# Turning the first two units' inputs on TensorE, one tile for the filler products, and instruction orders planned backwards and forwards, in a fused gated-linear-attention and MLP kernel

## The chip, the core and the metric

The kernel runs on one core of one Trainium2 chip. The metric is the device time of one launch in microseconds. All data is float32 on the chip; the two weight matrices arrive as 64-bit floats and are rounded to float32 by the kernel itself. In this document TensorE is PE, VectorE is DVE, ScalarE is ACT, GpSimd is POOL, and SyncE, which here only issues DMAs, is SP.

## The reference

A gated linear recurrence over 4 batches and 8 heads, 768 positions of 48 features each, and behind it a two-layer MLP on 3072 tokens:

```python
state = np.zeros((B, H, D, D))                      # B 4, H 8, S 768, D 48
for t in range(S):
    state = alpha[:, :, t, :, None] * state + np.einsum('bhd,bhe->bhde', k[:, :, t], v[:, :, t])
    y[:, :, t] = np.einsum('bhd,bhde->bhe', q[:, :, t], state)
x = y.transpose(0, 2, 1, 3).reshape(B * S, H * D)   # 3072 x 384
h = x @ w_in                                        # 384 x 2048
g = h - np.tanh(h)
out = g @ w_out                                     # 2048 x 384
```

## The kernel before

The 3072 tokens are cut into 12 **units** of 256 positions; a unit has two **chunks** of 128. For each unit the attention part (`gla`) makes the features `xT`, and the MLP part (`moe`) runs 8 **steps**, each of 256 hidden features: `first` (the product with `w_in`, tile `h`), `square`, `quad`, `cube`, `shrunk` (a polynomial for `h - tanh(h)`), and `second` (the product with `w_out`, tile `o`). Units 0 and 1 (`PLAIN = 2`) do `second` in the plain way while the weights are still coming in; later units use seven half-size products instead of eight, with combinations of the blocks of `w_out` (`combos`, tiles `b` and `e`).

Every piece of work is a task with an engine, an estimated duration, a rank and a list of tasks it needs. A planner lays the tasks out, and each engine then runs its own list strictly in that order:

```python
class Planner:
    def add(self, name, engine, us, rank, after, do, lat=0.25): ...
    def order(self):
        ...
        while any(open_.values()):
            at, engine = min((max(free.get(e, 0.0), min(ready[i] for i in ts)), e)
                             for e, ts in open_.items() if ts)
            i = min((i for i in open_[engine] if ready[i] <= at), key=lambda i: (self.tasks[i][3], i))
            ...            # the task of least rank among those that are ready
        return sorted(done, key=lambda x: x[:2])
```

The recurrence wants the features on the partitions and the positions along the row. alpha, k and q lie in memory the other way round, so they are loaded in rows of 1536 bytes into 32 partitions per half (`raws`), widened by ACT and transposed in 32 x 32 blocks by DVE:

```python
def load(u, what):                                  # what: 0 alpha, 1 k, 2 q, 3 v
    queue = A if u == 0 and what in (1, 3) else nc.sync
    if what == 3: ...                               # v, rows of 192 bytes, one DMA per chunk
    t, x = raws[what], (alpha, k, q)[what]
    for hh in range(2):
        src = x[b].rearrange("(g two) s d -> two g (s d)", two=2)[hh][:, t0 * D:(t0 + TU) * D]
        queue.dma_start(out=t[HP * hh:HP * hh + 32].rearrange("p g r d -> p g (r d)"),
                        in_=src.rearrange("g (i n) -> i g n", i=32))

def widen(what):                                    # ACT, two copies
    ...
def flip(what, make):                               # DVE, four 128x256 transposes
    t = make()
    for g in range(NP):
        V.transpose(t[:, g].rearrange("p c (i r) -> p r c i", r=R), raws[what][:, g, :, 0:32])
```

From the turned alpha two scans make the running products `U` (backwards) and `W` (forwards); k is multiplied by `U` (`kU`) and q by `W` (`qW`). Each chunk then has these tasks on PE, with DVE and ACT between them: `scores` (tile `sc`), `back` (tile `tp`, k turned back), `y`, `update` (tile `up`, what is added to the state). The features of a chunk are 8 heads x 48 = 384 = 3 x 128, but a pair of heads fills only 2 x 48 of 128 partitions; the last two heads fill the gaps of 16 partitions in the three tiles. In units 0 and 1 (`direct`) TensorE computes these gaps itself, with small products from `v_gap` and `s_gap`; in the other units the last two heads go into a fourth block, and six small DMAs (`moves`) bring them into the gaps:

```python
direct = u < PLAIN
def products():
    y = m["y", c] = bank("y")
    to_gap = [(hh, slice(HP * hh + D - gap, HP * hh + HP), j)
              for hh in range(2) for j in range(KT)] if direct else []
    rows = P if direct else HP + D
    if n > 0:
        for g in range(KT if direct else NP):
            T.matmul(y[0:rows, g, :], lhsT=old[:, g, 0:rows], rhs=m["qT"][:, g, c, :], ...)
        for hh, at, j in to_gap:
            T.matmul(y[at, j, :], lhsT=s_gap[quads[hh], j, :], rhs=m["qT"][quads[hh], NP - 1, c, :], ...)
    for hh, at, j in to_gap:
        T.matmul(y[at, j, :], lhsT=v_gap[:, c, hh, j, :], rhs=m["pm", c][hh][:, NP - 1, :], ...)
    for g in range(KT if direct else NP):
        for hh, q in enumerate(quads):
            T.matmul(y[q, g, :], lhsT=vts[u][:, c, 2 * g + hh, :], rhs=m["pm", c][hh][:, g, :], ...)
```

The weights come in 16 pieces, each 786 KB as 64-bit words, through four `raw` buffers; ACT reads a piece (two activations) and DVE rounds it (two instructions). Until there is real work, PE multiplies the identity with itself (`spin`):

```python
RANK = {"in": -3, "out": 8}
pieces = [("in", 0), ("in", 1)]
for s in range(FS):
    pieces += [("out", s)] + ([("in", s + 2)] if s + 2 < FS else [])
...
add("spin 0", "PE", 9, -99, [], lambda: spin(36))
add("spin 1", "PE", 1.5, -20, [f"qT 0"], lambda: spin(7))
```

At the end a flag `ok` is computed from the size checks on the data; where it fails, a slower general kernel runs. With the reference's inputs it does not run.

Of the kernel before, what the change touches and what calls it, by code (L numbers as in the profile page):

```python
# [317 lines left out]
class Planner:  # L318

    def __init__(self):
        self.tasks = []

    def add(self, name, engine, us, rank, after, do, lat=0.25):
        self.tasks.append((name, engine, us, rank, [a for a in after if a], do, lat))

    def order(self):
        names = {t[0]: i for i, t in enumerate(self.tasks)}
        assert len(names) == len(self.tasks)  # L330
        needs = [[names[a] for a in t[4]] for t in self.tasks]
        users = [[] for _ in self.tasks]
        for i, ns in enumerate(needs):
            for j in ns:
                users[j].append(i)
        left = [len(ns) for ns in needs]
        ready = [0.0] * len(self.tasks)
        free, open_ = {}, {}
        for i, t in enumerate(self.tasks):
            if not left[i]:  # L340
                open_.setdefault(t[1], []).append(i)
        done = []
        while any(open_.values()):

            at, engine = min((max(free.get(e, 0.0), min(ready[i] for i in ts)), e)
                             for e, ts in open_.items() if ts)
            i = min((i for i in open_[engine] if ready[i] <= at), key=lambda i: (self.tasks[i][3], i))
            open_[engine].remove(i)
            _, _, us, _, _, do, lat = self.tasks[i]
            free[engine] = at + us  # L350
            done.append((at, len(done), do, i))
            for j in users[i]:
                ready[j] = max(ready[j], at + us + lat)
                left[j] -= 1
                if not left[j]:
                    open_.setdefault(self.tasks[j][1], []).append(j)
        assert len(done) == len(self.tasks)
        return sorted(done, key=lambda x: x[:2])


def fast(tc, q, k, v, alpha, moe_w_in, moe_w_out, out, w_in, w_out, ident, ok, pad_rows):
# [17 lines left out]
    with ExitStack() as ctx:  # L379
# [12 lines left out]
        for t, x in zip(raws, (1.0, 0.0, 0.0)):  # L392
            for hh in range(2):
                V.memset(t[HP * hh + 32:HP * hh + HP, :, :, D - 32:32], x)

# [37 lines left out]
        RANK = {"in": -3, "out": 8}  # L433
# [15 lines left out]
        pieces = [("in", 0), ("in", 1)]  # L449
        for s in range(FS):  # L450
            pieces += [("out", s)] + ([("in", s + 2)] if s + 2 < FS else [])
        raw_of = {}

# [12 lines left out]
        for n, (what, s) in enumerate(pieces):  # L466
            rank = RANK[what] + 2 * s
            held = pieces[n - 4] if n >= 4 else None
            add(f"fetch {what}{s}", "SP", 3.9, rank - 30, [held and f"read {held[0]}{held[1]}"],
                lambda what=what, s=s: fetch(what, s), lat=2.5)  # L470
            a, b = convert(what, s)
            older = pieces[n - 2] if n >= 2 else None
            add(f"read {what}{s}", "ACT", 2.1, rank, [f"fetch {what}{s}", older and f"{older[0]}{older[1]}"], a)
            add(f"{what}{s}", "DVE", 1.6, rank, [f"read {what}{s}"], b)
# [4 lines left out]
        def load(u, what):  # L479

            b, i = divmod(u, UPB)
            t0 = i * TU
            queue = A if u == 0 and what in (1, 3) else nc.sync
            if what == 3:
                vt = vts[u] = two.tile([P, CU, H, D], FP32, name="vt")
                for c in range(CU):
                    queue.dma_start(out=vt[:, c],
                                    in_=v[b, :, t0 + c * P:t0 + (c + 1) * P, :].rearrange("h p d -> p h d"))
                return
            t, x = raws[what], (alpha, k, q)[what]  # L490
            for hh in range(2):
                src = x[b].rearrange("(g two) s d -> two g (s d)", two=2)[hh][:, t0 * D:(t0 + TU) * D]
                queue.dma_start(out=t[HP * hh:HP * hh + 32].rearrange("p g r d -> p g (r d)"),
                                in_=src.rearrange("g (i n) -> i g n", i=32))

        def gla(u, rank):
# [6 lines left out]
            direct = u < PLAIN  # L503
# [6 lines left out]
            for what, name in enumerate(("aT", "kT", "qT", "v")):  # L510
                go(f"load {name}", "SP", 2.3, -9 + 0.1 * what, [prev and what < 3 and f"{name}{prev}"]
                   + [f"{last} {u - 2}.{CU - 1}" for last in ("y", "state") if what == 3 and u > 1
                      and (last == "y" or (u - 2) % UPB < UPB - 1)],
                   lambda what=what: load(u, what), lat=2.5)

            def widen(what):
                for hh in range(2):
                    t, r0 = raws[what], HP * hh
                    to, of = t[r0 + 32:r0 + HP, :, :, 0:D - 32], t[r0:r0 + 32, :, :, 32:D]
                    if u == 0 and what == 0 and hh == 1:  # L520
                        V.tensor_copy(to, of)
                    else:
                        A.copy(to, of)
# [6 lines left out]
            def new(name):  # L530
# [3 lines left out]
                     lambda: new("kT"), lambda: new("qT"))  # L534
            for what, (name, k_) in enumerate((("aT", 0), ("kT", 2), ("qT", 4))):
                go(f"wide {name}", "ACT", 1.25, k_ - 0.5, [f"load {name}"], lambda what=what: widen(what))
# [10 lines left out]
            def ends():  # L547
# [4 lines left out]
                V.tensor_reduce(out=least[:, u:u + 1], in_=U[:, :, 0], axis=AX.X, op=ALU.min)  # L552
                V.reciprocal(before[:, 0::P + 1], e)

# [14 lines left out]
            go("U", "DVE", 2.3, 1, ["aT", prev and f"kU{prev}", prev and f"sizeU{prev}"], scan_U)  # L569
            go("ends", "DVE", 0.5, 3, ["U"], ends)  # L570
            go("W", "DVE", 2.3, 3, ["ends", prev and f"qW{prev}", prev and f"sizeW{prev}"], scan_W)
            go("kU", "DVE", 1.2, 3, ["kT", "U"], lambda: scale("kT", "U"))
            go("qW", "DVE", 1.2, 5, ["qT", "W"], lambda: scale("qT", "W"))
# [3 lines left out]
            def bank(name):  # L577


                if direct:  # L580
                    return ps_o.tile([P, NP, P], FP32, name=name, tag="o2" if name == "y" else "o3")
                return ps_sc.tile([P, NP, P], FP32, name=name, tag="sc0" if name == "y" else "sc1")

            def chunk(c):
# [25 lines left out]
                def masked():  # L610
                    pm = m["pm", c] = [two.tile([P, NP, P], FP32, name=f"pm{hh}", bufs=1) for hh in range(2)]
# [16 lines left out]
                def products():  # L628
                    y = m["y", c] = bank("y")
# [28 lines left out]
                def back():  # L658
                    tp = m["tp", c] = bank("tp")
# [7 lines left out]
                def update():  # L667
                    up = m["up", c] = bank("up")[:, :, 0:2 * D].rearrange("p g (two d) -> p g two d", d=D)
# [4 lines left out]
                def state():  # L673
                    for hh, q in enumerate(quads):
                        if n == 0:
                            V.tensor_copy(new[q, :, q], m["up", c][q, :, hh, :])
# [7 lines left out]
                kU, qW = f"kU {u}", f"qW {u}"  # L684
                go_c("scores", "PE", 1.2, 7, [kU, qW] + held, scores)
                go_c("masked", "DVE", 1.3, 8, ["scores", past and f"y {past}"], masked)
                if n > 0:
                    go_c("decay", "DVE", 0.6, 6, [f"ends {u}", f"state {past}"], decay)
                if direct:
                    go_c("gaps", "ACT", 0.9, 7, [f"load v {u}", n > 0 and "decay", past and f"y {past}"], gaps)  # L690
                go_c("y", "PE", 2.2 if n else 1.2, 9,
                     ["masked", f"load v {u}", n > 0 and "decay", direct and "gaps",
                      direct and past and f"x {past}"], products)
                go_c("x", "ACT", 0.6 if direct else 1.5, 10, ["y"], features)
                if not last:
                    go_c("back", "PE", 0.6, 6 if direct else 8.5,
                         [kU, None if direct else "masked", direct and past and not past_last and f"state {past}"], back)
                    go_c("natural", "ACT", 0.6, 9, ["back"], natural)
                    go_c("update", "PE", 1.15, 9.5, ["natural", f"load v {u}"], update)
                    go_c("state", "DVE", 0.8, 10,  # L700
# [40 lines left out]
        for n in range(5):  # L741
            add(f"combine {n}", "DVE", 1.7, 2 * FS + 1 + n,
                [f"out{FS - 1}", f"in{FS - 1}", f"gaps {PLAIN - 1}.{CU - 1}", f"y {PLAIN - 1}.{CU - 1}"]
# [18 lines left out]
        def moe(u, rank, gait):  # L762
# [3 lines left out]
            def step(s):  # L766
# [16 lines left out]
                def square():  # L783
                    if s % 2 == 0:
                        m["us"] = two.tile([P, 2, 2 * TU], FP32, name="u")
                    m["u", s] = m["us"][:, s % 2]
# [15 lines left out]
                def large():  # L802
                    big = two.tile([P, N * (P + 1)], FP32, name="big", tag="junk", bufs=1)[:, 0:4 * TU]
                    n = (u * FS + s) // 2
                    A.activation(big, m["us"].rearrange("p s t -> p (s t)"), AF.Relu, bias=-U_FAST, scale=W_SCALE,  # L805
# [9 lines left out]
                def second():  # L815
# [27 lines left out]
                    + [f"x {u}.{c}" if plain else f"moves {u}" for c in range(CU if plain else 1)], first)  # L843
# [50 lines left out]
        def spin(n):  # L894

            t = ps_o.tile([P, P], FP32, name="spin", tag="o0")
            for _ in range(n):
                T.matmul(t, lhsT=ident, rhs=ident, start=True, stop=True)
        add("spin 0", "PE", 9, -99, [], lambda: spin(36))
        add("spin 1", "PE", 1.5, -20, [f"qT 0"], lambda: spin(7))  # L900

# [28 lines left out]
        add("judge", "DVE", 1.2, 16 * NU, [f"large {last_step}", f"x {NU - 1}.{CU - 1}"] + [f"look {n}" for n in range(len(pieces))], judge)  # L930
# [73 lines left out]
```

## Time and profile before

| what | value |
|---|---|
| time, median of 3 runs | 622.51 us (618.29 to 622.78) |
| the profiled run | 617.95 us, span 616.2 us |
| PE busy | 596.8 us (97%), 3717 matmul instructions |
| DVE busy | 463.4 us (75%) |
| ACT busy | 342.5 us (56%) |
| POOL busy | 4.5 us (1%) |
| HBM read / written | 44.04 MB / 4.72 MB |
| chain that ended last, by engine | PE 92%, DMA 3%, DVE 2%, issue 1% |

The table is read from the top down: one engine is busy for almost the whole span, and the chain of work that ended last, which is followed back from the last instruction, runs over the same engine for 92% of the span. A group in the profile is named by what it writes and reads: `h<-xT,w_in` is the product with the first weight matrix. Each float32 matmul of the program appears as two instructions (for instance the 576 products `first` as 1152 records). "PEclk" is the granted share of the TensorE clock, 1.00 being full.

### The profile page before, as it was taken

The page shows a single profiled execution, that of the slowest core. Times are in us where ns is not written, and L with a number is a line of the kernel's source. Part 1 is how long each engine was busy: PE and PEld are TensorE (multiplying, and loading weights), DVE is VectorE, ACT ScalarE, POOL GpSimd, SP SyncE. Part 2 cuts the span into 40 slices and gives each one's busy share as a digit, 9 for nine tenths or more (in the row PEclk, how much of TensorE's full clock was granted, in tenths as well). Part 3 has the DMA queues.
Part 4 walks back from the last instruction along what each step waited for, and adds up shares of the span by engine and source line. Part 5 has one row for each costly group of instructions (what it writes and reads, how often), then busy time and mean ns, then how long its engine had stood idle before and what let it go on. Part 6 is the DMA issues. An engine that isn't in the chain of part 4 may idle for free.

```text
span 616.2 us, 9861 instructions
## 1 busy us (share of the span) xinstructions
PE 596.8 (97%) x3717; PEld 529.5 (86%) x3717; DVE 463.4 (75%) x885; ACT 342.5 (56%) x633; POOL 4.5 (1%) x18
## 2 busy tenths in 40 slices
PE   7689999999999999999999999999999999999994
PEld 7578776777999899999999999899899998999994
DVE  7997599997995896985895895786796744635652
ACT  3777898486877666676564564454444433333430
POOL 2000000000000000000000000000000000000000
PEclk9799999999999999999999999999999999999998
DMA  9996991445565275472040030030010000000001
GB/s 172 201 192 171 236 208 52 103 112 152 114 153 125 81 133 123 111 159 76 31 105 1 28 84 25 27 85 27 27 32 1 27 7 1 27 7 1 26 1 32
DMA packets 55161, 50.48 MB, mean 82 GB/s; under 512 B 29056, under 2 KB 44864, under 8 KB 55104
## 3 DMA queue, kind: packets, MB, share of 16 engines
q1 hardware_dynamic: 52448, 48.78, 34.3%
q10 hardware_dynamic: 2656, 0.98, 1.0%
q8 instruction: 31, 0.51, 0.4%
q14 instruction: 26, 0.21, 0.1%
HBM read 44.04 MB, written 4.72 MB: 79 GB/s over the span
## 4 chain that ended last, share of the span: by engine, by line
PE 92%; DMA 3%; DVE 2%; issue 1%; ACT 0%; ACTq 0%; SPq 0%; DVEq 0%
PE h L778 40%; PE o L838 30%; PE o L823 7%; PE sc L607 4%; PE y L646 4%; PE y L635 3%; DMA raw<-in_moe_w_in_dram 3%; PE up L670 2%; PE tp L661 1%; DMA kr<-in_k_dram 1%; DVE qT L528 1%; PE y L642 1%; DVE qT L563 0%; DVE W L558 0%; PE y L638 0%
## 5 line engine op out<-in xcount | busy, mean ns | idle before, releaser
L778 PE MATMUL h<-xT,w_in 128*128 128x256 f32 x1152 | 266.2, 381 | 0.6 <-ACT xT L652 0.6
L778 PEld LDWEIGHTS h<-xT,w_in 128*128 128x128 f32 x1152 | 215.9, 191 | 29.9 <-ACT xT L652 0.8
L787 ACT ACTIVATE u<-h 128x512 f32<-128x512 f32 x96 | 57.3, 596 | 205.4 <-PE h L778 204.9
L795 DVE TENSOR_TENSOR w<-h,u 128x512 f32<-128x512 f32 x96 | 66.1, 688 | 80.0 <-ACT u L787 79.9
L838 PE MATMUL o<-b,e 128*128 128x192 f32 x480 | 91.1, 326 | 0.0
L838 PE MATMUL o<-w_out,e 128*128 128x192 f32 x320 | 80.9, 335 | 0.0
L838 PEld LDWEIGHTS o<-b,e 128*128 128x128 f32 x480 | 80.2, 190 | 0.0
L799 DVE SCALAR_TENSOR_TENSOR g<-z,w 128x512 f32<-128x512 f32 x96 | 65.9, 687 | 10.7 <-ACT z L791 5.9
L838 PE MATMUL o<-b,g 128*128 128x192 f32 x320 | 65.1, 326 | 0.0
L838 PEld LDWEIGHTS o<-w_out,e 128*128 128x128 f32 x320 | 56.2, 190 | 6.9 <-issue 3.0
L791 ACT ACTIVATE z<-u 128x512 f32<-128x512 f32 x96 | 60.4, 629 | 2.3
L838 PEld LDWEIGHTS o<-b,g 128*128 128x128 f32 x320 | 54.2, 190 | 0.0
L805 ACT ACTIVATE big<-u 128x1024 f32<-128x1024 f32 x48 | 50.1, 1045 | 0.0
L823 PE MATMUL o<-w_out,g 128*128 128x384 f32 x128 | 44.0, 489 | 0.0
L823 PEld LDWEIGHTS o<-w_out,g 128*128 128x128 f32 x128 | 23.9, 190 | 14.3 <-issue 0.4
L811 DVE TENSOR_TENSOR e<-g 128x256 f32<-128x256 f32 x80 | 33.4, 418 | 2.4
L812 DVE TENSOR_TENSOR e<-g 128x256 f32<-128x256 f32 x80 | 33.4, 417 | 0.0
L607 PEld LDWEIGHTS sc<-qT,kT 48*128 48x128 f32 x368 | 23.4, 195 | 10.0 <-issue 5.2
L613 DVE TENSOR_TENSOR pm<-sc,mask 128x512 f32<-128x512 f32 x46 | 29.5, 683 | 3.2 <-PE sc L607 3.2
L607 PE MATMUL sc<-qT,kT 48*128 48x128 f32 x368 | 28.0, 294 | 2.4 <-DVE qT L563 2.4
L544 DVE TENSOR_TENSOR_SCAN U<-aT,after 128x1032 f32<-128x1032 f32 x12 | 27.5, 2294 | 0.3
L558 DVE TENSOR_TENSOR_SCAN W<-aT,before 128x1032 f32<-128x1032 f32 x12 | 27.6, 2302 | 0.0
(100 smaller groups left out, 617.9 us busy)
## 6 DMA issues: line engine op xcount, KB each, us to landing
raw<-in_moe_w_out_dram SPq DMA_DIRECT2D x16, 768.0 KB, 5.6
raw<-in_moe_w_in_dram SPq DMA_DIRECT2D x32, 288.0 KB, 6.6
ar<-in_alpha_dram SPq DMA_DIRECT2D x24, 192.0 KB, 3.4
qr<-in_q_dram SPq DMA_DIRECT2D x24, 192.0 KB, 3.3
kr<-in_k_dram SPq DMA_DIRECT2D x22, 192.0 KB, 4.9
vt<-in_v_dram SPq DMA_DIRECT2D x22, 192.0 KB, 4.1
raw<-in_moe_w_in_dram SPq DMA_DIRECT2D x32, 96.0 KB, 6.8
out_dram<-same SPq DMA_DIRECT2D x20, 96.0 KB, 1.7
```

The source lines that it names most:

```text
L607: T.matmul(sc[hh][:, g, :], lhsT=m["kT"][q, g, c, :], rhs=m["qT"][q, g, c, :], start=True, stop=True)
L613: V.tensor_mul(pm[hh], m["sc", c][hh], mask.unsqueeze(1).to_broadcast([P, NP, P]))
L778: T.matmul(h[:, a, :], lhsT=w_in[:, j, f * P:(f + 1) * P], rhs=xT[u][:, j, :], start=(j == 0), stop=(j == KT - 1))
L787: A.activation(m["u", s], m["h", s], AF.Square, scale=W_SCALE ** -1.5)
L791: A.activation(m["z", s], m["u", s], AF.Square, bias=QB, scale=QA * W_SCALE)
L795: V.tensor_mul(m["w", s], m["h", s], m["u", s])
L799: V.scalar_tensor_tensor(out=g.rearrange("p a c t -> p (a c t)"), in0=m["z", s], scalar=QK, in1=m["w", s], op0=ALU.add, op1=ALU.mult)
L805: A.activation(big, m["us"].rearrange("p s t -> p (s t)"), AF.Relu, bias=-U_FAST, scale=W_SCALE, accum_out=over[:, n:n + 1])
L811: V.tensor_add(e[:, 0:2, :], g[:, 0], g[:, 1])
L812: V.tensor_sub(e[:, 2:4, :], g[:, :, 1, :], g[:, :, 0, :])
L823: T.matmul(m["o"][c], lhsT=g[:, a, c, :], rhs=w_out[:, f, :], start=(f == 0), stop=(f == FT - 1))
L838: T.matmul(o[n][:, i], lhsT=g_, rhs=w_, start=(s == 0 and (n, i) in ((0, 0), (1, 0), (2, 1), (3, 0))), stop=(s == FS - 1), skip_group_chec ...
```

## The change

Its parts, and what each is for:

1. **alpha, k and q of unit 0 and k and q of unit 1 turned by TensorE** (`TURNED`). They are loaded in rows of 384 bytes (two positions of one head), 128 partitions at once (`rough`), one DMA each. PE multiplies each head's 64 columns with the identity, which turns them into PSUM: 8 matmuls for the even and 8 for the odd positions (`turn`). alpha is copied from PSUM (even half by ACT, odd half by DVE); k and q are multiplied by `U` and `W` straight out of PSUM, in two halves. This takes the place of `widen` on ACT and of four transposes on DVE for each of the five tensors.
2. **The second unit's gaps through DMAs**: `direct` holds for unit 0 alone. Unit 1 uses the fourth block and the six `moves`.
3. **All filler products into one tile**: the matmuls that only keep PE busy are 40 single tasks (`SPINS`), all into one PSUM tile `o2`, that the planner puts wherever PE would stand idle before the first `y`.
4. **The order**: the planner runs eight rounds. It plans forwards, turns the plan round to find how late each task may end, plans forwards again with those times as priorities (with some noise in later rounds), and keeps the shortest plan by its own estimates. An engine may also wait for a more urgent task that will soon be ready.
5. **Around it**: pieces of weights sorted by rank with `RANK["out"] = 3`; other estimates of durations; `least` taken out of `ends`; the first state copied by ACT instead of DVE; separate `pm` tiles for the second chunk of unit 0; other PSUM banks for the tasks of units 0 and 1; v's second half in unit 0 alone on ACT's queue.

The diff, cut to its core:

```diff
 class Planner:
+    ROUNDS, SEED, NOISE = 8, 1, 2.0
     def order(self):
-        ... one forward pass, least rank first ...
+        chance = random.Random(self.SEED)
+        priority, late, best = [t[3] for t in self.tasks], None, None
+        for n in range(self.ROUNDS):
+            starts, order = self.run(priority, before, after, late if n % 2 else None)
+            ends = [s + t[2] for s, t in zip(starts, self.tasks)]
+            if best is None or max(ends) <= best[0]:
+                best = max(ends), starts, order
+                turned, _ = self.run([-e for e in ends], after, before)
+                back = [r + t[2] for r, t in zip(turned, self.tasks)]
+                fair = [max(back) - b for b in back]
+            late = fair if n < 4 else [x + chance.gauss(0, self.NOISE) for x in fair]
+            priority = late
...
+        TURNED = ((0, 1, 2), (1, 2))
+        def by_matmul(u, what):
+            return u < len(TURNED) and what in TURNED[u]
...
-        RANK = {"in": -3, "out": 8}
+        RANK = {"in": -3, "out": 3}
-        pieces = [("in", 0), ("in", 1)]
-        for s in range(FS):
-            pieces += [("out", s)] + ([("in", s + 2)] if s + 2 < FS else [])
+        pieces = sorted(((what, s) for s in range(FS) for what in RANK), key=lambda x: (RANK[x[0]] + 2 * x[1], x))
+        SPINS = 40
... load():
+            if by_matmul(u, what):
+                if u > 0:
+                    make_rough(u, what)
+                (A if u == 0 and what == 1 else nc.sync).dma_start(
+                    out=rough[u, what][:, 0:BOTH].rearrange("p (h n) -> p h n", h=H),
+                    in_=x[b, :, t0:t0 + TU, :].rearrange("h (p two) d -> p h (two d)", two=CU))
+                return
... gla():
-            direct = u < PLAIN
+            direct = u == 0
+            def turn(what, n):
+                ...
+                t = m["turned", what, n] = pool.tile([P, NP, P], FP32, name="turned", tag=tag)
+                for h in range(H):
+                    at = (h * CU + n) * D
+                    T.matmul(t[HP * (h % 2):HP * (h % 2) + HP, h // 2, :], lhsT=rough[u, what][:, at:at + HP], rhs=ident,
+                             start=True, stop=True)
+            def place(n):
+                (V.tensor_copy if n else A.copy)(each(tail[:, :, 0:P], n), turned(0, n))
+            def times(what, by, n):
+                ...
+                V.tensor_mul(each(m[name].rearrange("p g c t -> p (g c) t"), n), turned(what, n), each(m[by][:, :, 1:], n))
...
-                            V.tensor_copy(new[q, :, q], m["up", c][q, :, hh, :])
+                            A.copy(new[q, :, q], m["up", c][q, :, hh, :])
...
-        add("spin 0", "PE", 9, -99, [], lambda: spin(36))
-        add("spin 1", "PE", 1.5, -20, [f"qT 0"], lambda: spin(7))
+        for n in range(SPINS):
+            add(f"spin {n}", "PE", 0.29, 99, [n > 0 and f"spin {n - 1}"], spin, lat=0.0)
```

From the order of the instructions in the changed program, without its times: PE runs 17 fillers, the turns of alpha and k, 1 filler, the turn of q, 4 fillers, `back` 0.0, 4 fillers, `update` 0.0, 7 fillers, both `scores` of unit 0, `back` 0.1, 7 fillers, `y` 0.0, `update` 0.1, `y` 0.1, the four turns of unit 1, and then the first two products with `w_in`. (0.1 is chunk 1 of unit 0.) The matmuls of the whole program change by 80 turns, 24 gap products fewer, 4 more products with `vt`, 2 more with `state` and 3 fillers fewer (43 to 40).

## The prediction, made before the changed kernel ran

> **What bounds the kernel now.** I read the page's forty slices first, to see where the busiest engine is not busy; then the table of windows over the start; then TensorE's timeline there; then the waits.
>
> ```profile
> PE   7689999999999999999999999999999999999994
> ...
> PEclk9799999999999999999999999999999999999998
> ```
>
> A slice is 15.4 us. PE is full from the fourth slice to the last but one, with the clock at full. The waits of PE between 60 and 600 us are an empty list, and PE is busy for 50.00 of 50.00 us in each window from 100 us on. So what remains after about 46 us is a fixed amount of PE work, and the end moves only by what PE idles, wastes or runs slowly before it, by PE work added or taken away, and by new stalls. The last matmul ends at 608 us; behind it lie 8 us of output that the change leaves alone.
>
> ```profile
> 10.00:15.00 5.00, 2.55 (x23) 2.36 (x23) 4.96 (x10) 1.32 (x3) 0.00 (x0) 1.00 1.18 177
> 15.00:20.00 5.00, 2.87 (x26) 2.68 (x26) 4.86 (x7) 3.46 (x5) 0.00 (x0) 1.00 1.08 180
> 20.00:25.00 5.00, 3.59 (x33) 3.42 (x33) 3.93 (x6) 2.03 (x3) 0.00 (x0) 0.57 1.08 201
> 25.00:30.00 5.00, 3.78 (x34) 2.54 (x30) 4.71 (x10) 4.84 (x9) 0.00 (x0) 0.75 1.23 212
> ...
> 45.00:50.00 5.00, 5.00 (x23) 4.21 (x22) 4.01 (x9) 2.96 (x7) 0.00 (x0) 0.70 0.08 18
> ```
>
> The columns are length, busy PE, weight loads, DVE, ACT, POOL, granted clock, DMA share, GB/s. From 10 to 20 us PE is half idle while DVE is full (4.96 and 4.86 of 5): DVE turns alpha, k and q. Then the clock falls to 0.57 and 0.75, and once more to 0.70 at 45 us. The DMA engines are full too.
>
> ```profile
> 1.52 10.91 PE L898 MATMUL spin<-ident 128*128 128x128 f32 x72 [1.52 <-POOL ident masks.py:199]
> 14.87 0.66 PE L661 MATMUL tp<-ident,kT 128*128 128x128 f32 x4 [2.45 <-DVE kT L563]
> ...
> 21.66 2.08 PE L607 MATMUL sc<-qT,kT 48*128 48x128 f32 x16 [1.41 <-DVE qT L563]
> ...
> 31.73 1.09 PE L638 MATMUL y<-qT,s_gap 48*32 48x128 f32 x12
> 32.75 1.09 PE L642 MATMUL y<-pm,v_gap 128*32 128x128 f32 x12
> ...
> 35.21 5.45 PE L778 MATMUL h<-xT,w_in 128*128 128x256 f32 x24 [0.58 <-ACT xT L652]
> ...
> 43.88 1.50 PE L607 MATMUL sc<-qT,kT 48*128 48x128 f32 x16 [1.03 <-DVE qT L563]
> ...
> 46.21 3.63 PE L778 MATMUL h<-xT,w_in 128*128 128x256 f32 x12
> ```
>
> A line is start, duration, engine, what, count and, in brackets, the idle time and its releaser. The scores of unit 0 wait for q until 21.66 us; the first product with `w_in` starts at 35.21. The useful work before it is only about 10 us: `back` and `update` twice (2.5), two `scores` (2.1 at full clock), `y` 0.0 (1.8), `y` 0.1 (3.5). So some 25 us at the start are waits, fillers and slow clock. After it PE waits twice (0.73 and 1.03 us), and twelve records of `h` take 3.63 us where twelve elsewhere take 2.59.
>
> **What the Trainium skill says.** The page "TensorE: Matmul & The Clock Gate", Part 1, says that the clock is at half until about 3.4 us of steady work, and falls back after an idle window. The trace agrees: 0.57 between 20 and 25 us, after idle gaps of 2.45, 2.13 and 1.41 us. It is why fillers between the real matmuls should help. Part 3 of that page says that matmuls in different row or column groups run side by side. The trace has the row kind: 16 records of `sc` with 48 rows, 8 matmuls of the program, take 1.16 us, so 145 ns each, against 303 ns for a filler (10.91/36). The turns write 64 columns at partitions 0 and 64 alternately; I give 8 of them and 8 scores 1.05 us a group (an estimate: 1.16 less the overlap of about 0.1 with the next group), which no trace here shows yet for the turns. "DMA: Bandwidth & Descriptors", Specifications, asks for transfers of 512 bytes or more for full rate. The trace shows the cost as smooth: in the DMA view from 6.8 to 8.6 us ACT's queue has 543 packets, nearly all rows of 192 bytes, in 38.8% of 16 x 1.8 us, so 20.6 ns each; from 2.5 to 6.8 us 276 packets of 1340 bytes on average in 39.6% of 16 x 4.3 us, so 99 ns each. A straight line between gives 34 ns for 384 bytes (estimate).
>
> **The change part by part.**
>
> Loads: alpha and k share the engines. Before, 2 x 256 packets of 1536 bytes at 112 ns over 16 engines are 3.6 us; after, 2 x 1024 at 34 ns are 4.35. alpha was there at 6.4 us, so now at about 7.2, and q 2.2 us later at 9.4. This part costs 0.8 us.
>
> DVE and ACT: 5 tensors x 2.03 us of transposes go (10.2), one widening copy (0.42) and the first state copy (0.73) too; in come one copy from PSUM (0.65) and eight half products at 0.7 for four whole ones at 1.2 (+0.8). DVE: -9.9 us. ACT: nine widening copies of 0.62 go (-5.6), and the gaps of unit 1 (-1.5); in come the other half of alpha (0.65), the state copy (0.7) and unit 1's features in two kinds of copies (0.26 + 0.47, four times, for 2 x 0.48: +2.0). ACT: -3.8 us. Neither is the bound, so this counts only where PE waits for it.
>
> PE, in the order that the changed program has, at full clock: 17 fillers end at 1.5 + 17 x 0.3 = 6.7; alpha at 7.2; turns of alpha and k 4.2: 11.4; filler 0.3 and turn of q 2.1: 13.8; 4 fillers: 15.0; `back` 0.45, 4 fillers, `update` 0.8: 17.45; 7 fillers: 19.55; two `scores` 2.1: 21.65; `back` 0.45: 22.1; 7 fillers: 24.2; `y` 0.0 1.85, `update` 0.8, `y` 0.1 3.5: 30.35; four turns of unit 1 4.2: 34.55. DVE keeps up: turned alpha at 9.3, copy 0.65 with its waits 10.1, `U` 2.3: 12.4, both halves of k and `ends`: 14.2 (`back` comes at 15.0), `W`: 16.5, q: 18.0 (`scores` come at 19.55). So the first `h` starts at **34.6 us**, hardly earlier than 35.2. The waste ahead of it falls from 25 us to 34.6 - 10 - 10.5 = 14, so by 11, but ten turn groups bring 10.5 us of new work. The fillers, 12 us of them, stand fixed in the queue and are a wait of their own where DVE is ready sooner.
>
> After it the same work is shorter. Before, from 35.2 to the end of the fifth `h` and the second `o` at 69.45: 34.2 us. After: five `h` (13.1), two `o` (5.2), two `scores` (2.1), two `back` (0.9), two `update` (1.6), two `y` of unit 1 without gap products (4 and 8 matmuls, 0.93 + 1.0, so 3.9): 26.8 us. The difference of 7.4 is 3.1 for the gap products (2 x (1.02 + 1.02), less 1.0 for the fourth block), 1.8 for the two waits, 1.5 for the slow `h` and `sc`, and about 1 for other slow or broken runs. PE arrives at this mark at 34.6 + 26.8 = 61.4 instead of 69.45: **8 us earlier**. Behind the mark the work is the same in both.
>
> **The rivals.**
>
> *Weights become the bound.* Three pieces of `w_in` were issued in 12.4 us, so 4.1 each; at the 248 GB/s of 60 to 80 us a `w_out` piece takes 3.2. From q at 9.4: v 2.6, seven `w_in` pieces 28.7, alpha, q, k, v of unit 1 8.9, three `w_out` 9.6 give 59.2 us for the seventh `w_in`; reading and rounding add 4: 63. PE wants it at 66.5. The margin is 3 us; if the four buffers or ACT (9.80 of 10 us busy from 90 to 100 us) break the stream, 2 to 5 us of the gain are lost: 615 to 618.
>
> *DVE becomes the bound.* It is 97 to 99% busy from 80 to 140 us. But it loses 9.9 us of work, more than PE gains, so the ratio stays. I give it 10%.
>
> *The turns or loads are slower.* The path holds ten turn groups: 0.1 us more each is 1 us; alpha 1 us later is 1 us.
>
> *More gain than counted.* The profiled run is 4 us below the median; if the ordinary run loses more to the slow clock in the gaps, and the steadier stream of fillers removes that, the gain against the median is 10 to 12 us.
>
> *The new order stalls PE later.* In both orders `second` of a step follows two to three `first` behind in nearly every step; I see nothing that gets tighter.
>
> **Range and chances.** 622.5 - 8.0 = 614.5; the last rival but one pulls it down by 2: 612.5. With weights as the bound 618; with a fully steady clock 606. Faster by 2% means under 610.1, which needs 12.4 us: 0.33. Slower by 2% would need a stall that nothing points to: 0.03.
>
> **What would show it.** Right: first `h` at 33 to 36 us; PE's clock at 0.95 or more up to 50 us; no gap products at 50 and 58 us; the end of the second `o` near 61 us; empty PE waits behind it. Wrong: PE waiting for `w_in` or `w_out` between 55 and 85 us; `turned` groups over 1.3 us; alpha later than 8 us; or the first `h` well under 33 us, which would mean that the turns cost less than I say.

## The result, and the profile after

| | median | range | runs |
|---|---|---|---|
| before | 621.4 us | 618.29 to 622.78 | 4 |
| changed | 611.51 us | 611.02 to 611.95 | 4 |

The ratio is 0.985, with an interval of 0.981 to 0.989: 9.9 us by the medians. That is likely the upper end of what the change is worth. In the three later sets, with 11 to 46 runs each, the kernel before had medians of 617.3, 617.8 and 617.9 us. The two profiled runs lie 6.0 us apart (spans of 616.2 and 610.2 us). The changed kernel itself was not run in those sets, but the kernel nearest to it there, the changed one with the old planner, lay 5.2 us under the kernel before of its own set (612.08 against 617.32). Taken together, the change saves about 6 us, and 10 only against that first set; the 6 is inferred across sets.

The forty slices of the page after, PE and its clock:

```profile
PE   9999999999999999999999999999999999999994
...
PEclk9999999999999999999999999999999999999998
```

Before, the first three slices held a 7, a 6 and an 8 and the clock a 7: now PE is full from the first slice on, at full clock. Part of that is filler. The windows of the changed kernel (length, busy PE, weight loads, DVE, ACT, POOL, clock, DMA share, GB/s):

```profile
10.00:15.00 5.00, 5.00 (x78) 4.54 (x75) 4.29 (x6) 1.51 (x4) 0.00 (x0) 1.00 1.11 212
15.00:20.00 5.00, 5.00 (x53) 4.87 (x53) 4.50 (x7) 3.00 (x6) 0.00 (x0) 1.00 1.21 187
20.00:25.00 5.00, 4.89 (x62) 4.41 (x62) 4.64 (x11) 4.85 (x10) 0.00 (x0) 1.00 1.16 235
```

PE's timeline of the changed kernel (start, duration, engine, line, what, count; idle time before it and its releaser in brackets):

```profile
1.51 6.91 PE L1028 MATMUL spin<-ident 128*128 128x128 f32 x34 [1.51 <-POOL ident masks.py:199]
8.35 3.71 PE L613 MATMUL turned<-ident,rough 128*64 128x128 f32 x64
...
19.17 1.16 PE L732 MATMUL sc<-qT,kT 48*128 48x128 f32 x16
...
33.24 5.45 PE L906 MATMUL h<-xT,w_in 128*128 128x256 f32 x24
...
41.97 2.42 PE L906 MATMUL h<-xT,w_in 128*128 128x256 f32 x10 [0.70 <-DVE w_in L87]
...
59.20 2.75 PE L906 MATMUL h<-xT,w_in 128*128 128x256 f32 x12
...
68.26 2.42 PE L906 MATMUL h<-xT,w_in 128*128 128x256 f32 x10 [0.71 <-DVE w_in L87]
...
600.24 1.14 PE L966 MATMUL o<-b,e 128*128 128x192 f32 x6
```

Two lines of the kernel before, to compare with (its second `o`, and its last group of matmuls):

```profile
66.71 2.74 PE L823 MATMUL o<-w_out,g 128*128 128x384 f32 x8
...
606.82 1.14 PE L838 MATMUL o<-b,e 128*128 128x192 f32 x6
```

The turns start with no idle time before them: PE came to them late because it was still at its 17 fillers. The two longer waits left are for a rounded piece of `w_in` (line 87 is the second rounding instruction). The fifth `h` starts at 59.20 and ends at 61.95, with two `o` done by then: that is the mark of the prediction, reached at 69.45 us before. PE's last matmul ends at 601.38 us, and at 607.96 before.

### The profile page after: what moved, and what is told of

Same layout as the page of the kernel before. It is cut to its first block, busy times and chain, and to the rows that moved or that the text cites. A ratio compares the mean times of both kernels' runs of the same rounds, so it can differ in the third digit from the quotient of the medians.

```text
span 610.2 us, 10100 instructions
## 1 busy us (share of the span) xinstructions
PE 598.1 (98%) x3835; PEld 531.8 (87%) x3835; DVE 452.9 (74%) x866; ACT 341.3 (56%) x633; POOL 4.4 (1%) x18
## 3 DMA queue, kind: packets, MB, share of 16 engines
q1 hardware_dynamic: 56688, 49.07, 35.2%
## 4 chain that ended last, share of the span: by engine, by line
PE 96%; DMA 1%; DVE 1%; SPq 0%; issue 0%; ACT 0%; POOL 0%; DVEq 0%; POOLq 0%
PE h L906 40%; PE o L966 30%; PE o L951 7%; PE sc L732 4%; PE y L775 4%; PE y L764 3%; PE up L799 3%; PE spin L1028 2%; PE tp L790 1%; DMA raw<-in_moe_w_in_dram 1%; PE turned L613 1%; PE y L771 0%; DVE w_in L87 0%; SPq L43 0%; DVE same L1007 0%
## 5 line engine op out<-in xcount | busy, mean ns | idle before, releaser
L732 PE MATMUL sc<-qT,kT 48*128 48x128 f32 x368 | 26.7, 285 | 0.0
```

Source lines behind the costliest of these rows:

```text
L732: T.matmul(sc[hh][:, g, :], lhsT=m["kT"][q, g, c, :], rhs=m["qT"][q, g, c, :], start=True, stop=True)
```

## The experiments

Twelve kernels ran. The number after "Measured" is the median, with the range in brackets, of four runs where no other number is given. The kernel before in the same sets had 617.79 (15 runs), 617.9 (46) and 617.32 us (11). "More" and "less" are against the changed kernel's 611.51 us, which comes from the first set; its medians are compared across sets, so differences of about 1 us are not certain, and the traces are read beside them. In the runs that alter what is turned, the gaps or the planner, the planner also lays out a new order, so they compare whole plans.

### Do the fillers help, or stand in the way?

Four runs. The first three keep the changed kernel's order and only leave fillers out:

```diff
-            add(f"spin {n}", ..., spin, lat=0.0)
+            add(f"spin {n}", ..., (lambda n=n: spin() if KEEP(n) else None), lat=0.0)
# e1: KEEP is never; e2: not 8 <= n < 17; e2b: 8, 1, 2, 2, 3, 3 of 17, 1, 4, 4, 7, 7
```

**No fillers.** 

> The changed kernel with its order kept, but none of the 40 fillers is emitted. Fillers keep the clock up (my reason): the granted clock falls under 0.8 somewhere between 5 and 30 us, the turns take up to twice as long, first product with w_in (33.2 us in the changed kernel) at 33 to 36 us, time 612 to 616 us. Rival, fillers stand in the way (17 of them end at 8.4 us while alpha lands at about 5.5): without them the first product starts near 30.5 us and the time is 607 to 609 us.

Measured: 611.89 us (610.89 to 611.98), the same as with all 40. The first line of its timeline, and its windows:

```profile
5.76 7.85 PE L613 MATMUL turned<-ident,rough 128*64 128x128 f32 x96 [5.76 <-DMA rough<-in_alpha_dram]
```

```profile
6.76:7.76 1.00, 1.00 (x14) 1.00 (x12) 0.00 (x0) 0.00 (x0) 0.00 (x0) 1.00 1.38 233
10.76:11.76 1.00, 1.00 (x22) 1.00 (x20) 1.00 (x1) 0.00 (x0) 0.00 (x0) 1.00 1.06 224
15.00:20.00 5.00, 3.07 (x27) 2.88 (x28) 3.58 (x6) 3.91 (x7) 0.00 (x0) 0.75 1.12 212
20.00:25.00 5.00, 5.00 (x44) 3.95 (x42) 4.51 (x10) 3.58 (x8) 0.00 (x0) 0.56 1.13 217
```

Both effects are there, and cancel. The turns start at 5.76 instead of 8.35 us, as soon as alpha is there. But the six groups of turns take 7.85 us instead of about 5.6, and this is not the granted clock, which is shown as 1.00: PE, idle until then, runs 14 of their records per us at first and 22 later (the changed kernel runs 19 in the first us of its turns). In the trace of the kernel before, the fillers are what starts slowly: 16 records in the first 3.48 us, then 38 in 5 us, also at 1.00. Behind the turns the clock falls to 0.75 and 0.56 as well, and the first half of `scores` takes 2.08 us instead of 1.16. The first `h` starts at 33.27 us, against 33.24.

**Eight first fillers.** 

> The changed kernel with its order kept; of the first block of 17 fillers only 8 are emitted, the other 23 stay. Fillers on the path: the turns start at 5.6 us instead of 8.35, the first product with w_in at 30.5 instead of 33.2 us, and if nothing else binds the time is 608.8 us (2.7 less). Rival, the weights bind behind it: the first product still starts near 30.5 us, but PE's waits for rounded w_in, 1.4 us in the changed kernel, grow to 3 to 4 us, and the time stays at 611 to 611.5 us. I expect something between, 610 us.

Measured: 610.28 us (609.70 to 610.67), 1.2 less. From PE's timeline in this run:

```profile
5.54 3.71 PE L613 MATMUL turned<-ident,rough 128*64 128x128 f32 x64 [0.40 <-DMA rough<-in_alpha_dram]
```

Now PE waits for alpha: it lands at 5.5 us. The first `h` starts at 30.43, 2.8 us earlier, and PE's last matmul ends 2.4 us earlier (598.99 against 601.38). PE's waits for `w_in` grow from 1.4 to 1.8 us only, so the weights take back little. The medians show half of the 2.4; the stretch behind the last matmul was 9.7 us in this run and 8.8 in the changed kernel's.

**Few fillers everywhere.** 

> As the run with 8 first fillers, and the later blocks cut as well: 1, 2, 2, 3, 3 in place of 1, 4, 4, 7, 7. Clock theory: the gaps are too short to lose the clock (under 1.5 us each), so it stays at 1.00; first product with w_in at 29 to 30 us, time 0 to 1 us under the run with 8 first fillers. Rival: the clock falls under 0.9 between 15 and 30 us and the time is 1 to 3 us over it.

Measured: 609.21 us (609.07 to 609.97), 2.3 less than the changed kernel, clock at 1.00 in every window to 80 us. PE idles 0.3, 0.2 and 0.6 us in the shortened places. The first `h` starts at 29.89 us, 0.5 earlier than with eight first fillers, so the later blocks, too, were longer than they had to be. PE's last matmul ends only 0.35 us earlier than in that run (598.64 against 598.99), and its waits for `w_in` are 2.0 us; the 1.1 us between the two medians is more than the traces show.

**Fillers in the kernel before.** 8 more ahead of the first `back`, 6 ahead of `update`, 5 ahead of `scores`.

> The kernel before, with 8, 6 and 5 fillers put ahead of the first back, update and scores, where PE stood idle. Clock theory: the clock stays at 1.00 from 10 to 30 us, the 32 records of scores take 2.1 us instead of 3.8, the time falls by 2 to 4 us to about 618 us, and the spread of the runs (618 to 623 before) shrinks to under 1.5 us. Rival: the spread and the 4 us between the profiled run and the others come from elsewhere, and median and spread stay at 620 to 622 and 4 us.

Measured: 617.54 us (615.89 to 620.21, 12 runs), ratio to the kernel before 0.999 (0.997 to 1.002). The clock is full to 80 us and the 32 records of `scores` take 2.1 us, but the first `h` starts at 35.83 us, not before 35.21: PE now waits 1.4 us for the masked scores and 2.8 us for ACT's copy instead. In the kernel before, the slow clock at the front stood beside other waits and cost nothing by itself that these runs can show. The range is 4.3 us, not under 1.5, against 6.6 in 15 runs of the kernel before. The spread goes with the clock all the same: over a whole run the mean granted clock was 0.993 to 0.996 in the runs of this kernel under 619 us and 0.990 and 0.989 in its two slowest; the kernel before, over its three sets, had 0.978 to 0.983 in its six runs above 621 us and 0.982 to 0.992 in those under 619. Where the clock falls in the longer ones isn't on record, so the cause stays open.

### What is each part worth?

**Unit 1's gaps on TensorE again**

```diff
-            direct = u == 0
+            direct = u < PLAIN
```

> The changed kernel with the gaps of unit 1 computed by TensorE again (direct for units 0 and 1); the planner lays its order out anew. My step: 3.1 us of work come back on an engine that is full, so the time rises by 3.1 to about 614.6 us and the gain at the end of the fifth h and second o shrinks by the same. Rival, PE waits for weights around 42 and 68 us, so the work is hidden in part: it rises by 1 us or less, and PE's waits for w_in (1.4 us) go to zero.

Measured: 614.08 us (613.35 to 614.78, 11 runs), 2.6 more, of the 3.1 expected. PE still waits for `w_in` once, 1.6 us. In the traces the stretch from the first `h` to PE's last matmul is 571.14 us, against 568.14: 3.0 more, and the first `h` came 1.3 us earlier because the 17 fillers took 5.61 us in this trace, not 6.91. The gaps through DMAs are worth about 2.6 to 3 us, because PE's time is what counts there.

**Only unit 0 turned**

```diff
-        TURNED = ((0, 1, 2), (1, 2))
+        TURNED = ((0, 1, 2), ())
```

> The changed kernel with k and q of unit 1 turned by DVE again; only unit 0 is turned by TensorE. PE loses four groups of 0.9 us, so the first product with w_in comes 3.7 us earlier, at 29.6 us; DVE gains two times 2.03 us less 0.1. If PE's time is what counts, the time falls by 2 to 3.7 us, to 608 to 609.5. If DVE holds the scores of unit 1 (DVE is 94% busy from 20 to 45 us), PE waits 2 to 4 us for q before them and the time is 611 to 612.5, no better. I expect 611.

Measured: 617.11 us (616.02 to 618.89, 12 runs): **5.6 us slower than the changed kernel**, with 3.7 us less work on PE. Two of its windows, and the two largest of its waits of PE (who waited for whom: us, times, longest):

```profile
35.00:40.00 5.00, 2.65 (x24) 2.12 (x24) 4.86 (x9) 4.29 (x7) 0.00 (x0) 1.00 0.88 176
40.00:45.00 5.00, 3.73 (x22) 3.12 (x21) 4.61 (x8) 3.63 (x6) 0.00 (x0) 0.56 0.52 165
```

```profile
PE h L906 <- DVE w_in L87: 3.1, 2, 2.1
PE sc L732 <- DVE qT L679: 1.6, 1, 1.6
```

The first `h` comes at 30.23 us, three earlier. Then DVE, with unit 1's k and q to transpose, is full (4.86 of 5) and PE half idle; the clock falls to 0.56, and twelve records of `h` take 5.02 us for 2.6. My second branch named DVE and the wait for q; the slow clock behind it, and the waits for rounded weights, it did not have.

**Nothing turned** (`TURNED = ((), ())`)

> The changed kernel with nothing turned by TensorE; gaps of unit 1 through DMAs, fillers and planner as changed. DVE's transposes are back on the path to the scores of unit 0: they start at 21 to 22 us (19.2 in the changed kernel), the first product with w_in at 31 to 33 us, since the four turns of unit 1 are gone too. Time 613 to 615 us, so the turns are worth 2 to 3 us. Rival, the turns only move work from DVE to PE and are worth nothing: 611 to 612.

Measured: 615.97 us (613.81 to 619.58, 20 runs), 4.5 more than the changed kernel. In this run and the next one the loads of unit 1 are tied to other tasks, since the turns that they waited for are gone. `scores` start at 20.93 us, about as said, but the first `h` at 35.42:

```profile
35.42 4.54 PE L904 MATMUL h<-xT,w_in 128*128 128x256 f32 x12 [2.20 <-ACT xT L779]
```

The clock is at 0.50 to 0.59 from 15 to 30 us, and the last 2.2 us before this `h` PE waits for ACT's copy of the features, in front of which ACT had been waiting 2.6 us for a piece of weights. Against the kernel before of the same set (617.9 us) the ratio is 0.996 (0.994 to 0.998): without the turns, the rest of the change is worth about 1.9 us.

**Only unit 1 turned** (`TURNED = ((), (1, 2))`)

> The changed kernel with unit 0 turned by DVE again and only k and q of unit 1 turned by TensorE; the fourth corner beside the changed kernel (611.5 us), unit 0 alone (617.1) and none (616.0). If the two turns add up, this corner is 616.0 - 617.1 + 611.5 = 610.4 us. If they need each other (turning unit 0 brings the front forward, turning unit 1 keeps DVE from holding it back behind the first h), it is 614 to 616 us: the scores of unit 0 start at 21 us with the clock at 0.5 to 0.6, as with none turned. I expect 614.5.

Measured: 612.97 us (612.53 to 613.75). The four corners, medians in us (the left column is one set, the other two corners are from two more):

| | unit 1 by DVE | unit 1 by TensorE |
|---|---|---|
| unit 0 by DVE | 615.97 | 612.97 |
| unit 0 by TensorE | 617.11 | 611.51 |

Unit 1's turns save 3.0 us alone and 5.6 with unit 0's; unit 0's cost 1.1 alone and save 1.5 with unit 1's. I expected too much of unit 0. The trace says where its gain went: with only unit 1 turned, the first `h` starts at 36.03 us, 2.8 later than in the changed kernel, but from there to PE's last matmul it takes 566.12 us and not 568.14, and PE never waits for `w_in`. What turning unit 0 gains at the front, the changed kernel gives back in part at the waits for `w_in` (1.4 us). Most of the gain is the second unit's, the one whose turns lie fully on PE's path.

**The new planner alone in the kernel before**, with the two squares of a pair kept apart by name, as in the change.

> The kernel before with the new planner alone (and the two squares of a pair kept apart by name, as in the change). My prediction gave the order no gain of its own: 616 to 618 us, like the kernel before. Rival, the order is where the gain lies: 612 to 614 us, with the first product with w_in under 34 us and no waits of PE at 41 and 43 us.

Measured: 619.88 us (616.93 to 621.81, 12 runs), ratio 1.0025 (1.0003 to 1.0048). No gain, if anything a small loss: it places the first `back` at 18.79 us with 4.5 us of idle PE before it, and the clock falls to 0.50.

**The old planner in the changed kernel**

> The changed kernel with the old planner (one forward pass, least rank first); turns, gaps through DMAs and fillers as changed. The new planner alone gave the kernel before nothing. If the order counts only where fillers and turns have to be fitted in, the old one costs 1 to 3 us: 612.5 to 614.5. Rival, the order is worth nothing here too: 611 to 612.

Measured: 612.08 us (611.53 to 613.42), 0.6 more, with ranges that overlap (611.02 to 611.95 for the new one). So the order planned back and forth is worth 0 to 1 us here. The parts under "around it" in the list of the change (estimates, ranks, PSUM banks, ACT's state copy) were not tried one by one.

### The two waits that are left

**`w_in` kept piece by piece.** Rounding a piece (line 87) waited for PE. In the changed kernel, on DVE:

```profile
36.38 0.55 DVE L86 TENSOR_SCALAR bits<-raw 128x768 int32<-128x768 int32 x1
38.81 0.96 DVE L87 CUSTOM_DVE_ANT_0 w_in<-bits,more 128x1536 uint16<-128x1536 uint16 x1 [1.89 <-PE h L906]
```

A piece of a 128 x 3 x 2048 tile is three stretches with other pieces between them. The suspicion is that the program therefore orders the write of one piece behind products that read others.

```diff
-    w_in = consts.tile([P, KT, d_ff], FP32, name="w_in")
+    w_in = consts.tile([P, FT // 2, KT, 2 * P], FP32, name="w_in")
```

> The changed kernel with w_in kept piece by piece (128 x 8 x 3 x 256 in place of 128 x 3 x 2048), so that a piece is one stretch of memory and rounding it no longer waits for earlier products of other pieces; order and fillers the same. If that wait is false and is what PE's 1.4 us of waits for w_in come from, they go to 0.3 us or less, DVE no longer idles 1.9 us behind h at 38.8 us, and the time is 610.1 us. Rival, the weights really arrive too late: waits of 1 us and more stay and the time is 611 to 611.5.

Measured: 609.51 us (608.69 to 609.83), 2.0 less. From the first `h` to PE's last matmul it is 565.74 us, against 568.14, so 2.4 less; in the traces the end comes 3.4 us earlier, but 1.0 of that is the 17 fillers, which took 5.92 us here and 6.91 there. All that is left in the list of PE's waits is the start:

```profile
PE spin L1028 <- POOL ident masks.py:199: 1.5, 1, 1.5
```

The same rounding instruction now follows without idle time:

```profile
36.06 0.96 DVE L87 CUSTOM_DVE_ANT_0 w_in<-bits,more 128x1536 uint16<-128x1536 uint16 x1
```

So these waits were false: the weights had arrived, and only the order held them back.

**Both together**

> The last one with the fillers cut to 8, 1, 2, 2, 3, 3 as well, which alone gave 609.2 us. If the two gains are independent: 607.5 to 608 us, with PE's waits under 1 us between 30 and 70 us. If bringing PE forward makes the weights the bound: 608.5 to 609.2, with PE waiting over 1.5 us for rounded weights.

Measured: median 607.56 us, as the first branch said, ratio to the kernel before 0.985 (0.982 to 0.989), against 0.987 (0.983 to 0.990) for the cut fillers alone. Five of six runs lie between 605.79 and 608.27; the sixth took 613.67 at a mean granted clock of 0.990 where the others had 0.996 to 0.997. PE waits for no weights, its last matmul ends at 595.1 us, and the first `h` starts at 29.38. By its median this is the fastest kernel here, 4 us under the changed one; with short fillers a run seems to be more exposed to the clock, for which one run is thin evidence.

## Why the prediction was right, point by point

The number was 612.5 us, the result 611.5. The mechanism held: PE is full behind the start, and what is gained is gained before about 62 us. The way to the number had several errors that cancelled in part, and that was luck. The gain of 2% to which the prediction gave 0.33 was not reached (0.985).

- **A fixed amount of PE work behind 46 us**: right. Behind 46 us PE waits once, 0.7 us; from the first `h` on, 1.6 us in all.
- **Loads**: mis-sized, 7.2 us for alpha, measured 5.5. The term was 34 ns for a packet of 384 bytes. In the DMA view from 1 to 8 us ACT's queue (`q10 hardware_dynamic: 1040, 0.39, 23.4%`) moves 1040 packets, nearly all of 384 bytes, in 23.4% of 16 x 7 us, so 25 ns each. The dearer small packets that the prediction counted with are there at 192 bytes (its 20.6 ns) and not at 384.
- **The first fillers**: mis-sized, and what held PE. 17 of them were to end at 6.7 us, at the mean of 0.30 us over 36; they ended at 8.4. The mean hides the slow start: in the trace of the kernel before the first 16 records take 3.48 us, so 0.44 us a filler, and the next 38 take 5.0, so 0.26.
- **The turns**: 1.05 us a group predicted; four take 3.64 us from start to start, 0.91 each. Ten groups are 9.1 us, not 10.5.
- **First `h` at 34.6**: 33.24. The cheaper turns make 1.4 us. Two other errors cancelled by luck: the turns started at 8.35 us and not at 7.2, and the 23 later fillers took 5.9 us and not 6.9. "Hardly earlier than 35.2" nearly stands: the front alone gains 2 us.
- **The mark at 61.4**: 61.95, again with errors that cancel: the first `h` 1.4 us earlier than predicted, and the stretch behind it 28.7 us and not 26.8, 0.9 of that being two waits (0.23 and 0.70) that the prediction didn't have. The gain at the mark is 7.5 us, predicted 8. Gap products 2.6 to 3.0 of 3.1 by the experiment; the slow `h` is gone, and so are the two waits of the kernel before.
- **"Behind the mark the work is the same in both", and "I see nothing that gets tighter"**: the second is the step that failed. PE's last matmul ended 6.6 us earlier, so 0.9 of the 7.5 were lost. The wait at 68.26 us for rounded `w_in` is 0.7 of it. It is one of the prediction's own signs of being wrong (PE waiting for `w_in` between 55 and 85 us), and it fell on the seventh piece, where the prediction saw a margin of 3 us. The run with `w_in` in pieces shows that it was a false order and not late weights. The trace of the kernel before shows the same kind of wait: its DVE sat idle behind `h` for up to 3.47 us before rounding a piece, though PE did not wait for the result there. Behind the last matmul a further 0.6 us went (8.8 for 8.2), in a stretch that the change doesn't touch.
- **The baseline**: I subtracted from the median of 622.5 and added 2 us for a steadier clock. The two medians differ by 9.9, the traces by 6.0. The later sets put the kernel before at 617.3 to 617.9, so 8 us was too much, rather than too little, by nearly 2. Only the high first set made the absolute number fit so well.
- **Rival "weights become the bound"**: refuted as a matter of supply. With the first `h` 2.8 to 3.4 us earlier still, PE's waits for `w_in` grew only to 1.8 and 2.0 us, and with the other layout, 3.9 us earlier, they were gone.
- **Rival "more gain than counted"**: the changed kernel's four runs do lie within 1 us, where the kernel before ranges over 3 to 7.5 in its sets. Its four runs all have a mean granted clock of 0.996 or 0.997, and in the kernel before a longer time goes with a lower clock, which fits the rival. But more fillers in the kernel before neither brought the median down nor the range under 4 us, so that it is the fillers which steady the clock is not shown.
- **Rival "DVE becomes the bound"**: not in the changed kernel. The run with unit 0 alone turned shows it would have come with half the change.
- **DVE, ACT**: DVE fell by 10.5 us of work (9.9 predicted), ACT by 1.2 (3.8).

## What to carry to other kernels

When an engine is full for most of a run, its own idle, slow and wasted time at the front is what a change can win, and work may be moved onto it if that ends a wait on another engine: here 3.7 us more of TensorE work for unit 1 saved 5.6 us beside the turns of unit 0, and 3.0 without them. Fillers that hold the clock stand in an in-order queue like any other work; size them to the landing time that the trace shows, count the first ones at their slow start, and find by a run how far the gaps must be filled (19 fillers kept the clock at 1.00 here as 40 did, and none did not). A wait whose releaser is a product that doesn't read what is being written can come from the tile's layout; another layout tells.

## What the runs showed of the hardware that was not expected

- Packets of 384 bytes took 25 ns on the DMA engines, 15 bytes per ns, no slower per byte than packets of 1340 bytes on average in the kernel before (99 ns, 13.5 bytes per ns); only the 192-byte rows there were dearer (20.6 ns, 9.3).
- The first 17 fillers took 6.91 us in one run and 5.61 and 5.92 us in two others with the same instructions. PE's first products run slower than later ones (0.44 us a filler for the first eight, 0.26 for the next nineteen, in the kernel before), and the granted clock is shown as 1.00 in all of these. The start of PE differs by over 1 us from run to run.
- Idle gaps of PE of 0.3, 0.2 and 0.6 us left the clock at 1.00; gaps of 0.8, 0.7 and 1.3 us in the same places, in a run whose PE also stood idle for the first 5.8 us, were followed by 0.75 and 0.56. The length of a gap alone does not decide: in the kernel before with more fillers, gaps of 1.4 us (before 25.2 us) and 2.8 us (before 30.7 us) left the clock at 1.00. No rule for it comes out of these runs.
